# Attention and the transposes of q on quarters of the TensorE array, with a new order in the front of a fused attention, MoE and MLP kernel

## The chip, the cores and the metric

The kernel runs on one core of a Trainium2 chip. Its time is the device time of one execution in microseconds, the median of several runs. Engine names: TensorE (PE in the rows, its weight loads PEld), VectorE (DVE), ScalarE (ACT), GpSimd (POOL), SyncE (SP), which here only starts transfers.

## What is computed

Three layers in a row. A linear attention without softmax, with a norm over each head's 64 outputs; its result, 2304 rows of 512, goes into a mixture of 8 experts, two for each row, and that into an MLP with a squared ReLU.

```python
kv = einsum('bhsd,bhse->bhde', k, v)           # 4 batches, 8 heads, 576 rows, 64 columns
out = einsum('bhsd,bhde->bhse', q, kv)
x = out / sqrt(mean(out * out, -1) + 1e-6) * g_norm
logits = x @ w_gate                            # x as 2304 x 512
noisy = logits + log1p(exp(x @ w_noise)) * noise
top2 = the two largest of 8; their softmax weights
y[rows of e] += weight * (relu(x @ w1[e]) @ w2[e])
out = (s * relu(y @ w_in) ** 2 + b) @ w_out
```

## The kernel before

The order of every engine's instructions is the order of the program: nothing moves them. The front (everything up to line 747) does the attention and the gating of the first half of the rows; the main part (from line 1041) does the expert and MLP products in steps, each an `l1` (lines 789 to 791), an `l2` (813 to 815) and the side work of that step.

The 2304 rows lie in 18 tiles of 128, each made of two halves of 64 rows (`TILES`), tiles 0 to 8 from batches 0 and 1, tiles 9 to 17 from batches 2 and 3. Two tiles make a chunk, and the last of each half is alone: ten chunks, numbered 0 to 9, chunks 4 and 9 with one tile.

For a batch, `kv` multiplies k and v in pieces of 64x64, alternating over the quarters of the array, and sums over the halves in two PSUM tiles. The sums are copied to `kvc` (326, 327), and from there to the diagonal blocks of `kvbd` (`kv_diag`), which was set to zero before. `mfold_a` transposes `kvc`, and `mfold_b` multiplies the result by the gate weights, so that 16 gate columns stand behind the 64 of each head (358, 360). Thus the attention product of a tile gives 8 heads of 80 columns.

For a tile, `q_tr` brings q's columns onto the partitions by products with the identity (380) and copies the result to `qT`, even tiles on ScalarE (386), odd ones on VectorE (384). `att` multiplies it by `kvbd`, two heads at once over 128 partitions, 160 columns (397). `evict` copies the result to `x` (411). `squares` and a sum on VectorE give each head's sum of squares (418, 421). `inv_rms` takes Ln and Exp on ScalarE (429, 430). `norm` makes one Newton step on it, scales the gate columns, sums them over the heads into the logits `lg`, and scales the rest to `xn` (439 to 450). `put_rows` writes `xn` to DRAM. Chunk c's norm is issued in the round of chunk c+1.

Loads of q, k, v, the stores of `xn` and the loads of weights are all started from SP in program order. `advance(n)` loads and splits weight units up to n: `w1h` and `w2h` on ScalarE (141, 148), `w1l` on VectorE (143), `w2l` on GpSimd (149).

When the first half's logits are there, `chain` holds the generator `gating(0)`. Each `tick()` placed in the front's code runs it on to its next `yield`, a yield of n waiting n ticks: the noise (472 to 476), two choices of the best expert in three steps each, the ranks by a product, one-hots (513), the table of the first 256 rows of expert 0 (519, `idx_e` 523), two gathers of rows on GpSimd (182), and `put_x`, which transposes them (367) and splits them into `xh` on ScalarE and `xl` on VectorE (370, 371). With these, group 0's first `l1` can run. The gating of the second half lies in the first steps of the main part.

Of the kernel before, what the change touches and what calls it, by code (L numbers as in the profile page):

```python
# [21 lines left out]
def kernel(  # L22
# [188 lines left out]
    small = [(fps, "tr", 4)]  # L211
# [25 lines left out]
    def warm(n):  # L237
        ps = small_ps([P, KC, P])
        for _ in range(n):
            nc.tensor.matmul(ps, lhsT=onesb, rhs=onesb[:, None, :].to_broadcast([P, KC, P]), start=True, stop=True)  # L240
# [72 lines left out]
    def kv(b, a0=0, a1=2):  # L313
# [10 lines left out]
        if a1 == 2:  # L324
            KVP[b] = kvc = pool.tile([P, 2, 2, D], F32, name="kvc", bufs=1)
            nc.scalar.activation(kvc[:, :, 0], ps[0], AF.Copy)
            nc.vector.tensor_copy(kvc[:, :, 1], ps[1])

    def kv_diag(b):
        kvc = KVP[b]  # L330
        for m in range(2):
            r = slice(m * D, (m + 1) * D)
            dst = kvbd[b][r, :, :, m, :D]
            if m == 0:
                nc.scalar.activation(dst, kvc[r], AF.Copy)
            else:
                nc.vector.tensor_copy(dst, kvc[r])


    def mfold_a(b):  # L340
        kvc = KVP[b]
# [5 lines left out]
        kv_diag(b)  # L347
        KVP[b] = kvT

    def mfold_b(b):  # L350
# [4 lines left out]
        for m in range(2):  # L355
            r = slice(m * D, (m + 1) * D)
            if m == 0:
                nc.scalar.activation(kvbd[b][r, :, :, m, D:], pm[r, :, m], AF.Copy)
            else:
                nc.vector.tensor_copy(kvbd[b][r, :, :, m, D:], pm[r, :, m])  # L360
# [14 lines left out]
    def q_tr(t):  # L375
        pt = small_ps([P, 2, 2, P])
        for i, (b, j) in enumerate(TILES[t]):
            for a in range(2):
                for m in range(2):
                    nc.tensor.matmul(pt[m * D:(m + 1) * D, i, a, :], lhsT=KQV[b, "q"][:, 2 * a + m, j, :], rhs=ident,  # L380
                                     start=True, stop=True)
        qT = pool.tile([P, 2, 2, P], F32, name="qT", bufs=3)
        if t % 2:
            nc.vector.tensor_copy(qT, pt)
        else:
            nc.scalar.activation(qT, pt, AF.Copy)
        QT[t] = qT

    def att(t):
        qT = QT.pop(t)  # L390
        ps = fps.tile([P, 2, 512], F32, name="att", bufs=2)
        pv = ps[:, :, :H // 2 * HW_].rearrange("p a (m i c) -> p a m i c", m=2, i=2)
        for a in range(2):
            for i in range(2):
                for s_, (b, _) in enumerate(TILES[t]):
                    r = slice(s_ * HP, (s_ + 1) * HP)
                    nc.tensor.matmul(pv[r, a, :, i, :], lhsT=qT[:, s_, a, i * HP:(i + 1) * HP], rhs=kvbd[b][:, a, i],
                                     start=True, stop=True)
        AT[t] = ps[:, :, :H // 2 * HW_].rearrange("p a (h c) -> p a h c", h=H // 2)


    CHUNKS = []
    for t0 in (0, NT0):
        CHUNKS += [(t, min(2, t0 + NT0 - t)) for t in range(t0, t0 + NT0, 2)]

    def evict(c, i):
        t0, n = CHUNKS[c]
        if i == 0:
            XC[c] = (pool.tile([P, 2, H, HW_], F32, name="x", bufs=3),)
        x, = XC[c]  # L410
        nc.scalar.activation(x[:, i].rearrange("p (a h) c -> p a h c", a=2), AT.pop(t0 + i), AF.Copy)
        tick()

    def squares(c):
# [4 lines left out]
        ss = pool.tile([P, 2, H], F32, name="ss", bufs=3)  # L419
        tick()  # L420
        nc.vector.tensor_reduce(ss[:, :n], sq[:, :n], axis=AX, op=OP.add)
        tick()
        XC[c] = (x, ss)

    def inv_rms(c):
        x, ss = XC[c]
        n = CHUNKS[c][1]
        y = pool.tile([P, 2, H], F32, name="iv", bufs=3)
        nc.scalar.activation(y[:, :n], ss[:, :n], AF.Ln, scale=1.0 / D, bias=eps)
        nc.scalar.activation(y[:, :n], y[:, :n], AF.Exp, scale=-0.5)  # L430
        XC[c] = (x, ss, y)

    def norm(c):
        x, ss, y = XC.pop(c)
        t0, n = CHUNKS[c]
        x, ss, y = x[:, :n], ss[:, :n], y[:, :n]
# [31 lines left out]
    def gate_noise(g):  # L468
# [9 lines left out]
        yield 3  # L478
# [30 lines left out]
    def early_table(t0, t1, b0, b1, out, add=None):  # L509
# [5 lines left out]
        yield 6  # L515
# [11 lines left out]
    def gate_rank(g):  # L527
# [12 lines left out]
        if g == 0:  # L540
# [3 lines left out]
            yield 12  # L544
# [28 lines left out]
    def gating(g):  # L573
# [3 lines left out]
        yield 4  # L577
# [124 lines left out]
    for nm in "kv":  # L702
        load(2, nm)
    mfold_a(0)
    load(2, "q")
# [4 lines left out]
    KV_AT = {2: 1, 6: 2, 11: 3}  # L710
    LOADS = {3: (3, "kv"), 8: (3, "q")}

    for c, (t0, n) in enumerate(CHUNKS):
        for i in range(n):
            t = t0 + i
            att(t)
            if t - 1 in KV_AT:
                mfold_a(KV_AT[t - 1])
            if t + 2 < NT:
                q_tr(t + 2)  # L720
            if t - 1 in KV_AT:
# [6 lines left out]
            if t in LOADS:  # L728
                b, nms = LOADS[t]
                for nm in nms:  # L730
                    load(b, nm)
# [356 lines left out]
```

## Time and profile before

| | us |
|---|---|
| median of 3 runs | 992.24 (990.45 to 992.96) |
| the profiled execution, its own time | 993.61 |
| its span | 991.9 |
| TensorE busy | 950.9 (96%) |
| VectorE busy | 534.1 (54%) |
| ScalarE busy | 386.8 (39%) |
| GpSimd busy | 107.2 (11%) |

[...] The span is the time from the first to the last instruction; the execution's own time is 1.7 us longer.

### The profile page before, as it was taken

What the parts mean: (1) busy time and instruction counts of PE and PEld (TensorE: products, weight loads), DVE (VectorE), ACT (ScalarE), POOL (GpSimd) and SP (SyncE); (2) the same over time, 40 slices, a digit from 0 to 9 for tenths busy, and PEclk for the clock granted to TensorE, in tenths of its full rate; (3) what the DMA queues carried; (4) which work ended last, traced back from release to release, by engine and by line L of the source; (5) the groups of instructions that cost most, each with busy time, mean ns of one, the idle gap of its engine ahead of it and who ended that gap; (6) DMA issues with size and microseconds to landing.
All of it is one profiled execution on the core that took longest, in us unless ns stands there. A gap on an engine that the chain in (4) does not pass through costs nothing.

```text
span 991.9 us, 14894 instructions
## 1 busy us (share of the span) xinstructions
PE 950.9 (96%) x5874; PEld 822.8 (83%) x5875; DVE 534.1 (54%) x981; ACT 386.8 (39%) x685; POOL 107.2 (11%) x122
## 2 busy tenths in 40 slices
PE   7866999999999999999999999999999999999997
PEld 5755877989999999999999998788788878887885
DVE  2578776544676776767545455444443443444332
ACT  2554334234564555555435434222222322222221
POOL 2002325101000100100000121100110010000000
PEclk8995999999999999999999999999999999999999
DMA  9644577537476674764645541200130021001001
GB/s 333 244 164 168 175 218 239 171 107 234 138 220 215 222 272 153 228 219 155 216 142 199 170 143 50 63 1 11 32 86 1 22 74 32 1 1 43 1 1 42
DMA packets 99420, 129.14 MB, mean 130 GB/s; under 512 B 7920, under 2 KB 62192, under 8 KB 99344
## 3 DMA queue, kind: packets, MB, share of 16 engines
q1 hardware_dynamic: 91952, 108.03, 33.1%
q0 software_dynamic: 6176, 20.08, 6.9%
q8 instruction: 47, 0.77, 0.3%
q10 hardware_dynamic: 1216, 0.03, 0.1%
q14 instruction: 29, 0.24, 0.1%
HBM read 92.98 MB, written 35.13 MB: 129 GB/s over the span
## 4 chain that ended last, share of the span: by engine, by line
PE 76%; DVE 1%; ACT 1%; issue 0%; ACTq 0%
PE ph L790 13%; PE ph L791 13%; PE ph L789 12%; PE y L813 12%; PE y L814 12%; PE y L815 12%; PE sps L367 2%; DVE r L799 0%; ACT hh L801 0%; ACT r L798 0%; DVE xl L371 0%; DVE r L800 0%; DVE hl L802 0%; DVE rows L822 0%; ACT xh L370 0%
## 5 line engine op out<-in xcount | busy, mean ns | idle before, releaser
L790 PE MATMUL ph<-xl,w1h 128*128 128x320 f32 (+3 forms) x832 | 278.1, 334 | 2.9 <-DVE xl L371 2.7
L789 PE MATMUL ph<-xh,w1h 128*128 128x320 f32 (+3 forms) x832 | 277.7, 334 | 2.0 <-ACT xh L370 1.2
L791 PE MATMUL ph<-xh,w1l 128*128 128x320 f32 (+3 forms) x832 | 277.5, 334 | 0.0
L813 PE MATMUL y<-w2h,hh 128*128 128x512 f32 x608 | 242.4, 399 | 2.6 <-ACT hh L801 1.7
L815 PE MATMUL y<-w2h,hl 128*128 128x512 f32 x608 | 237.9, 391 | 0.0
L814 PE MATMUL y<-w2l,hh 128*128 128x512 f32 x608 | 237.7, 391 | 0.0
L790 PEld LDWEIGHTS ph<-xl,w1h 128*128 128x128 f32 x832 | 157.9, 190 | 18.6 <-DVE xl L371 5.1
L789 PEld LDWEIGHTS ph<-xh,w1h 128*128 128x128 f32 x832 | 158.0, 190 | 18.1 <-ACT xh L370 3.4
L791 PEld LDWEIGHTS ph<-xh,w1l 128*128 128x128 f32 x832 | 157.9, 190 | 9.9
L799 DVE SCALAR_TENSOR_TENSOR r<-ph,r 128x512 f32<-128x512 f32 (+1 forms) x80 | 51.0, 638 | 177.6 <-ACT r L798 176.1
L793 ACT ACTIVATE hh<-ph 128x320 fp32r<-128x320 f32 (+2 forms) x128 | 55.9, 437 | 230.6 <-PE ph L791 220.0
L794 DVE SCALAR_TENSOR_TENSOR hl<-ph,hh 128x320 fp32r<-128x320 f32 (+2 forms) x128 | 62.5, 490 | 142.3 <-ACT hh L793 136.2
L815 PEld LDWEIGHTS y<-w2h,hl 128*128 128x128 f32 x608 | 114.1, 188 | 25.7 <-DVE hl L802 0.6
L813 PEld LDWEIGHTS y<-w2h,hh 128*128 128x128 f32 x608 | 114.4, 188 | 23.8 <-ACT hh L801 2.4
L814 PEld LDWEIGHTS y<-w2l,hh 128*128 128x128 f32 x608 | 114.4, 188 | 20.3
L798 ACT ACTIVATE r<-ph 128x512 f32<-128x512 f32 (+1 forms) x80 | 44.3, 554 | 189.6 <-PE ph L791 183.9
L801 ACT ACTIVATE hh<-r 128x512 fp32r<-128x512 f32 (+1 forms) x80 | 47.1, 589 | 101.8 <-DVE r L800 97.9
L802 DVE TENSOR_TENSOR hl<-r,hh 128x512 fp32r<-128x512 f32 (+1 forms) x80 | 51.2, 639 | 52.5 <-ACT hh L801 50.3
L182 POOL DMA_INDIRECT rows<-xs,idx x35 | 34.9, 998 | 314.0 <-PE sps L367 176.5
L182 POOL DMA_INDIRECT rows<-ys,slot_i x36 | 34.8, 968 | 272.0 <-DVE rows L771 133.1
L143 DVE SCALAR_TENSOR_TENSOR w1l<-raw,gcol,w1h 128x512 fp32r<-128x512 f32 x64 | 47.8, 748 | 24.5 <-ACT w1h L141 19.9
L148 ACT ACTIVATE w2h<-raw 128x512 fp32r<-128x512 f32 x80 | 49.7, 621 | 2.3 <-DMA raw<-in_moe_w_dram 2.3
(166 smaller groups left out, 809.2 us busy)
## 6 DMA issues: line engine op xcount, KB each, us to landing
raw<-in_moe_w_dram SPq DMA_DIRECT2D x128, 256.0 KB
ys<-rows SPq DMA_DIRECT2D x40, 256.0 KB
c_raw<-in_moe_w_in_dram SPq DMA_DIRECT2D x16, 512.0 KB
c_raw<-in_moe_w_out_dram SPq DMA_DIRECT2D x16, 512.0 KB
wd<-c_fl SPq DMA_DIRECT2D x16, 512.0 KB
raw<-wd SPq DMA_DIRECT2D x32, 256.0 KB
ys<-zero SPq DMA_DIRECT2D x13, 512.0 KB
q<-in_q_dram SPq DMA_DIRECT2D x4, 1152.0 KB
```

Source lines behind the costliest of these rows:

```text
L148: nc.scalar.activation(h2, r2, AF.Copy)
L182: nc.gpsimd.indirect_dma_start(out=dst, out_offset=None, in_=src, in_offset=bass.IndirectOffsetOnAxis(ap=icol, axis=0))
L789: nc.tensor.matmul(ps[:, :wd], lhsT=w1h[:, c, :], rhs=xh[:, c, cs], start=c == 0, stop=False)
L790: nc.tensor.matmul(ps[:, :wd], lhsT=w1h[:, c, :], rhs=xl[:, c, cs], start=False, stop=False)
L791: nc.tensor.matmul(ps[:, :wd], lhsT=w1l[:, c, :], rhs=xh[:, c, cs], start=False, stop=c == KC - 1)
L793: nc.scalar.activation(hh[:, cs], ps[:, :wd], AF.Relu)
L794: nc.vector.scalar_tensor_tensor(hl[:, cs], ps[:, :wd], 0.0, hh[:, cs].bitcast(F32), op0=OP.max, op1=OP.subtract)
L799: nc.vector.scalar_tensor_tensor(r[:, :wd], ps[:, :wd], 0.0, r[:, :wd], op0=OP.max, op1=OP.mult)
L802: nc.vector.tensor_sub(hl[:, cs], r[:, :wd], hh[:, cs].bitcast(F32))
L813: nc.tensor.matmul(y, lhsT=hh[:, cs], rhs=w2h, start=f == 0, stop=False)
L814: nc.tensor.matmul(y, lhsT=hh[:, cs], rhs=w2l, start=False, stop=False)
L815: nc.tensor.matmul(y, lhsT=hl[:, cs], rhs=w2h, start=False, stop=f == nf - 1)
```

## The change

Four things. First, `att` and `q_tr` also work on 64x64 pieces: the state is kept as `kvg` without zero blocks, a product takes one head's 64 partitions and 80 columns, and the transposes take 64 rows of q each, so that each product of before becomes two. Second, `q_tr` does both tiles of a chunk, two chunks ahead, with one copy on ScalarE. Third, the copies of the key-value state move between the engines: both `kvc` copies and both fold copies are ScalarE's, and VectorE copies the sums straight from PSUM in `kv_put`. A part of the Newton step goes to GpSimd. Fourth, the round of a chunk has a new order, ticks and yields differ, and three weight units are split in the front instead of four. PSUM is shared out anew: two small tiles instead of four, and two banks for the transposes.

```diff
-    small = [(fps, "tr", 4)]
+    small = [(fps, "tr", 2)]
...
-    kvbd = []
-    for b in range(B):
-        t = pool.tile([P, 2, 2, 2, HW_], F32, name=f"kvbd{b}")
-        nc.gpsimd.memset(t, 0.0)
-        kvbd.append(t)
+    kvg = [pool.tile([P, 2, 2, HW_], F32, name=f"kvg{b}") for b in range(B)]
...
+            for i in range(2):
+                nc.scalar.activation(kvc[:, :, i], ps[i], AF.Copy)
+            KVP[b] = ps, kvc
+
+    def kv_put(b):
+        for i in range(2):
+            nc.vector.tensor_copy(kvg[b][:, :, i, :D], KVP[b][0][i])
...
-            if m == 0:
-                nc.scalar.activation(kvbd[b][r, :, :, m, D:], pm[r, :, m], AF.Copy)
-            else:
-                nc.vector.tensor_copy(kvbd[b][r, :, :, m, D:], pm[r, :, m])
+            nc.scalar.activation(kvg[b][r, :, :, D:], pm[r, :, m], AF.Copy)
...
+    def q_tr(c):
+        if c >= NCH:
+            return
+        t0, n = CHUNKS[c]
+        pt = fps.tile([P, 2, 2, 2, 2, HP], F32, name="qtp", bufs=1)
+        for u in range(n):
+            for s_, (b, j) in enumerate(TILES[t0 + u]):
+                for a in range(2):
+                    for m in range(2):
+                        for i in range(2):
+                            r = slice(i * HP, (i + 1) * HP)
+                            nc.tensor.matmul(pt[m * D:(m + 1) * D, i, u, s_, a, :], lhsT=KQV[b, "q"][r, 2 * a + m, j, :],
+                                             rhs=ident[r, r], start=True, stop=True)
+        qT = pool.tile([P, 2, 2, 2, 2, HP], F32, name="qT", bufs=3)
+        fl = "p i u s a t -> p i u (s a t)"
+        nc.scalar.activation(qT.rearrange(fl)[:, :, :n], pt.rearrange(fl)[:, :, :n], AF.Copy)
+        QT[c] = qT
...
+                    for m in range(2):
+                        r = slice(m * D, (m + 1) * D)
+                        nc.tensor.matmul(pv[s_ * HP:(s_ + 1) * HP, m, a, i, :], lhsT=QT[c][r, i, u, s_, a, :],
+                                         rhs=kvg[b][r, a, i, :], start=True, stop=True)
...
+    def sums(c):
+        x, sq = XC[c]
+        n = CHUNKS[c][1]
+        ss = pool.tile([P, 2, H], F32, name="ss", bufs=2)
+        nc.vector.tensor_reduce(ss[:, :n], sq[:, :n], axis=AX, op=OP.add)
+        w = pool.tile([P, 2, H], F32, name="iw", bufs=2)
+        nc.gpsimd.tensor_scalar(w[:, :n], ss[:, :n], -0.5 / D, -0.5e-6, op0=OP.mult, op1=OP.add)
         tick()
...
-        nc.vector.tensor_scalar(ss, ss, -0.5 / D, -0.5e-6, op0=OP.mult, op1=OP.add)
         nc.vector.tensor_mul(u, y, y)
+        nc.vector.tensor_mul(u, u, w)
         tick()
-        nc.vector.tensor_mul(u, u, ss)
...
-        yield 3
+        yield 2
...
-        yield 6
+        yield 3
...
-            yield 12
+            yield 11
...
-        yield 4
+        yield 2
...
-    KV_AT = {2: 1, 6: 2, 11: 3}
-    LOADS = {3: (3, "kv"), 8: (3, "q")}
+    KV_AT = {3: 1, 7: 2, 11: 3}
...
-        for i in range(n):
-            t = t0 + i
-            att(t)
-            if t - 1 in KV_AT:
-                mfold_a(KV_AT[t - 1])
-            if t + 2 < NT:
-                q_tr(t + 2)
-            if t - 1 in KV_AT:
-                mfold_b(KV_AT[t - 1])
-            if c and i == 0:
-                inv_rms(c - 1)
-            evict(c, i)
-            if t in KV_AT:
-                kv(KV_AT[t])
...
-            if c and i == n - 1:
-                norm(c - 1)
-            if 12 <= t < 16:
-                advance(t - 11)
-            elif t == 11:
-                advance(0)
...
-        squares(c)
-        put_rows()
+        new = None
+        for u in range(n):
+            att(c, u)
+            evict(c, u)
+            if u == 0:
+                inv_rms(c - 1)
+            if t0 + u in KV_AT:
+                new = KV_AT[t0 + u]
+                kv(new)
+        squares(c)
+        q_tr(c + 2)
+        if new:
+            kv_put(new)
+            mfold_a(new)
+        norm(c - 1)
+        put_rows()
+        sums(c)
+        if new:
+            mfold_b(new)
+        if c == 1:
+            for nm in "kv":
+                load(3, nm)
+        if c == 2:
+            load(3, "q")
+        if c and sum(CHUNKS[c - 1]) == NT0:
+            chain[:] = [gating(0), 0]
+        if c >= 6:
+            advance(c - 6)
```

## Rows read from the trace of the kernel before

**Rows 1.** Busy time by stretch: PE, PEld, DVE, ACT, POOL, granted clock, DMA share, GB/s.
```profile
14.00:61.00 47.00, 39.14 (x866) 35.23 (x864) 25.78 (x55) 23.55 (x50) 0.68 (x2) 0.96 0.77 279
61.00:96.00 35.00, 21.54 (x214) 16.67 (x206) 27.81 (x67) 16.74 (x33) 7.25 (x6) 0.67 0.43 142
96.00:991.90 895.90, 880.85 (x4643) 765.56 (x4643) 477.83 (x844) 344.96 (x600) 92.02 (x89) 0.99 0.38 119
```

**Rows 2.** Waits from 14 to 96 us: total us, times, longest.
```profile
ACT iv L429 <- DVE ss L421: 22.0, 8, 6.0
...
PE att L397 <- ACT x L411: 9.4, 5, 2.5
```

**Rows 3.** Timeline, an undisturbed round: start, us, engine, instruction, [idle before].
```profile
37.11 0.31 ACT L429 ACTIVATE iv<-ss,eps 128x16 f32<-128x16 f32 x1 [1.13 <-DVE ss L421]
...
38.03 0.17 DVE L440 TENSOR_TENSOR iu<-iv 128x16 f32<-128x16 f32 x1
...
40.75 1.22 DVE L421 TENSOR_REDUCE ss<-sq 128x16 f32<-128x1024 f32 x1
42.00 0.31 ACT L429 ACTIVATE iv<-ss,eps 128x16 f32<-128x16 f32 x1 [0.87 <-DVE ss L421]
```

**Rows 4.** Groups by line, 14 to 96 us: count, busy us, mean ns, idle before.
```profile
L411 ACT ACTIVATE x<-att 128x640 f32<-128x640 f32 x18 | 12.2, 690 | 0.0
...
L384 DVE COPY qT<-sps 128x512 f32<-128x512 f32 x9 | 6.2, 689 | 9.0 <-PE sps L380 9.0
L386 ACT ACTIVATE qT<-sps 128x512 f32<-128x512 f32 x9 | 5.4, 595 | 8.2 <-PE sps L380 8.2
```

**Rows 5.** Timeline of ScalarE, a square and two copies of a kv.
```profile
38.88 1.06 ACT L418 ACTIVATE sq<-x 128x1024 f32<-128x1024 f32 x1
...
43.05 0.27 ACT L326 ACTIVATE kvc<-sps 128x128 f32<-128x128 f32 x1
45.28 0.38 ACT L346 ACTIVATE kvT<-sps 128x256 f32<-128x256 f32 x1 [1.96 <-PE sps L344]
```

**Rows 6.** Timeline of TensorE: q_tr, att, kv.
```profile
24.19 1.09 PE L380 MATMUL sps<-ident,q 128*64 128x128 f32 x16 [0.46 <-DMA q<-in_q_dram]
...
35.15 1.28 PE L397 MATMUL att<-kvbd,qT 128*64 128x160 f32 x16
36.24 1.07 PE L380 MATMUL sps<-ident,q 128*64 128x128 f32 x16
...
40.42 2.33 PE L322 MATMUL sps<-v,k 64*64 64x64 f32 x144
...
74.02 2.40 PE L397 MATMUL att<-kvbd,qT 128*64 128x160 f32 x16 [2.52 <-ACT x L411]
```

**Rows 7.** Timeline, the noise of gating: its first and last operation.
```profile
58.68 0.25 ACT L472 ACTIVATE g<-lg 128x72 f32<-128x72 f32 x1
...
59.81 0.34 POOL L476 TENSOR_TENSOR g<-g,lg 128x72 f32<-128x72 f32 x1
```

**Rows 8.** Timeline of VectorE, gating and weights, and one GpSimd operation.
```profile
65.20 0.23 DVE L490 TENSOR_TENSOR g<-g,m_all 128x72 f32<-128x72 f32 x1
...
74.61 0.75 DVE L143 SCALAR_TENSOR_TENSOR w1l<-raw,gcol,w1h 128x512 fp32r<-128x512 f32 x1 [1.10 <-ACT w1h L141]
75.28 1.25 DVE L439 TENSOR_SCALAR ss<-ss 128x16 f32<-128x16 f32 x1
...
77.42 2.88 DVE L513 TENSOR_SCALAR ohe<-io,early 128x256 f16<-128x256 f16 x9
...
75.17 1.32 POOL L149 TENSOR_TENSOR w2l<-raw,w2h 128x512 fp32r<-128x512 f32 x1 [7.46 <-ACT w2h L148]
```

**Rows 9.** Timeline, the end of the front: gather, transposes, first product on xl.
```profile
88.05 1.08 POOL L182 DMA_INDIRECT rows<-xs,idx_e  x1 [0.17 <-DVE iu L440]
...
93.52 1.11 PE L367 MATMUL sps<-ident,rows 128*128 128x128 f32 x4 [0.52 <-DMA rows<-xs,idx_e]
...
96.04 0.58 PE L790 MATMUL ph<-xl,w1h 128*128 128x256 f32 x1
```

More of the change, by code (lines that the diff above doesn't have):

```diff
@@ L237, in warm @@
     def warm(n):
-        ps = small_ps([P, KC, P])
+        ps = fps.tile([P, KC, P], F32, name="warm", tag="att", bufs=2)
         for _ in range(n):
@@ L324, in kv @@
         if a1 == 2:
[L325 to L333, printed above, removed]
-            if m == 0:
-                nc.scalar.activation(dst, kvc[r], AF.Copy)
-            else:
-                nc.vector.tensor_copy(dst, kvc[r])
+            kvc = pool.tile([P, 2, 2, D], F32, name="kvc", bufs=1)
+            for i in range(2):
[4 more added lines that the diff above has]
+            nc.vector.tensor_copy(kvg[b][:, :, i, :D], KVP[b][0][i])
     def mfold_a(b):
-        kvc = KVP[b]
+        kvc = KVP[b][1]
         pt = small_ps([P, 2, P])
@@ L346, in mfold_a @@
         nc.scalar.activation(kvT, pt, AF.Copy)
-        kv_diag(b)
         KVP[b] = kvT
@@ L356, in mfold_b @@
             r = slice(m * D, (m + 1) * D)
-            if m == 0:
-                nc.scalar.activation(kvbd[b][r, :, :, m, D:], pm[r, :, m], AF.Copy)
-            else:
-                nc.vector.tensor_copy(kvbd[b][r, :, :, m, D:], pm[r, :, m])
+            nc.scalar.activation(kvg[b][r, :, :, D:], pm[r, :, m], AF.Copy)
     X = {0: tuple(gp.tile([P, KC, EB * P], F32R, name=n) for n in ("xh0", "xl0"))}
@@ L373, with att @@
     QT, AT, XC, XO = {}, {}, {}, []
[L375 to L392, printed above, removed]
+    CHUNKS = []
+    for t0 in (0, NT0):
+        CHUNKS += [(t, min(2, t0 + NT0 - t)) for t in range(t0, t0 + NT0, 2)]
+    NCH = len(CHUNKS)
+    def q_tr(c):
[15 more added lines that the diff above has]
+        QT[c] = qT
+    def att(c, u):
+        t = CHUNKS[c][0] + u
+        ps = fps.tile([P, 2, 512], F32, name="att", tag="att", bufs=2)
+        pv = ps[:, :, :H // 2 * HW_].rearrange("p m (a i c) -> p m a i c", a=2, i=2)
         for a in range(2):
@@ L395, in att, with evict @@
                 for s_, (b, _) in enumerate(TILES[t]):
[L396 to L406, printed above, removed]
+                    for m in range(2):
+                        r = slice(m * D, (m + 1) * D)
+                        nc.tensor.matmul(pv[s_ * HP:(s_ + 1) * HP, m, a, i, :], lhsT=QT[c][r, i, u, s_, a, :],
+                                         rhs=kvg[b][r, a, i, :], start=True, stop=True)
+        AT[t] = pv.rearrange("p m a i c -> p m a (i c)")
+    def evict(c, u):
         t0, n = CHUNKS[c]
-        if i == 0:
+        if u == 0:
             XC[c] = (pool.tile([P, 2, H, HW_], F32, name="x", bufs=3),)
-        x, = XC[c]
-        nc.scalar.activation(x[:, i].rearrange("p (a h) c -> p a h c", a=2), AT.pop(t0 + i), AF.Copy)
-        tick()
+        x = XC[c][0][:, u].rearrange("p (a m i) c -> p m a (i c)", a=2, m=2)
+        nc.scalar.activation(x, AT.pop(t0 + u), AF.Copy)
     def squares(c):
@@ L701 @@
     kv(0, 1, 2)
-    for nm in "kv":
+    kv_put(0)
+    for nm in "kvq":
         load(2, nm)
     mfold_a(0)
-    load(2, "q")
     q_tr(0)
```

30 lines of the change are left out of this document (14 added, 16 removed).

## The prediction

> **What bounds the kernel now.** I read the granted clock and span first, then busy time by stretch, then the waits, and last the engines' timelines of the front. Two stages with different limits stand out [rows 1]. From 96 us on TensorE is busy 880.85 of 895.9 us: the expert and MLP products run back to back, the change touches none of them, and so nothing is to be won there. Before 96 us it is busy 39.14 of 47.0 and then 21.54 of 35.0 us, at a mean granted clock of 0.67 in the second stretch. The front ends when the rows of group 0 are split into xh and xl and the first l1 product that reads xl starts, at 96.04 [rows 9]. What the change is worth is how far this moment moves; it then carries over one to one, as long as nothing behind it waits for something that didn't move too.
>
> In the front TensorE isn't the engine that ends last. ScalarE waits 22.0 us in all in front of inv_rms for VectorE's sums, and TensorE's att waits 9.4 us for the eviction that is queued behind that inv_rms [rows 2]. The undisturbed round of a chunk is a circle over two engines [rows 3]: sums end, Ln and Exp on ScalarE, norm on VectorE, the next sums, the next Ln. From Ln at 37.11 to Ln at 42.00 it takes 4.89 us: 0.92 to the first multiply of norm (38.03), 3.94 from there to the end of the sums (41.97). The qT copy, the kv copies, gating and the weight splits are queued in between and lengthen it.
>
> **The change part by part.**
> *Quarters.* Per tile, att was 16 instructions in 1.28 us and the transposes 16 in 1.07 us [rows 6], 2.35 together. Now each is 32 instructions on 64x64 pieces, of 80 and 64 columns. The nearest row is kv, which already runs in the same alternation of quarters: 144 instructions with 64 columns in 2.33 us, 16.2 ns each. That gives 32 x 16.2 = 0.52 us for the transposes and, scaled by the columns that are loaded and streamed (144/128), 0.58 us for att: 1.1 us for a tile, 2.2 for a chunk. Bounds: 2.2 at full clock, 4.4 at half (att took 2.40 us at 74.02, after 2.52 us of idling, against 1.28). The saving of some 1.25 us a tile, 22 us in all, is almost all off the path: in a round of 4.8 us TensorE was no bound, and it gets more idle time.
>
> [...]
>
> *Copies of q.* One ScalarE copy of 1024 columns for two tiles takes the place of alternating copies of 512, 0.689 us on VectorE and 0.595 on ScalarE [rows 4]. Its cost lies between 1.06 (the square of 1024 columns, [rows 5]) and 2 x 0.595 = 1.19; I take 1.06. VectorE loses 9 x 0.69 = 6.2 us, of which 5 x 0.69 = 3.5 lie after 61 us, where VectorE is the busiest engine (27.81 of 35 us, [rows 1]). ScalarE then has per chunk two evictions at 0.69, Ln (0.31, [rows 3]) and Exp (taken as 0.22), square and copy at 1.06: 4.0 us, inside the round, so its copies cost nothing while the round is VectorE's. The cover is thin (0.8 us), and gone in the three chunks with a kv.
>
> [...]
>
> *Key-value state.* The zeroed kvbd, its diagonal copies and one fold copy on VectorE go; ScalarE does both kvc copies (0.27 each, [rows 5]) and both fold copies; VectorE does the two kv_put copies of the same size, ahead of norm, while it waits for Ln and Exp. The long stop, VectorE standing in front of norm until the fold was copied, goes. In its place kv_put waits for kv alone, and norm is queued behind it.
>
> *Orders.* evict(c,0) now goes ahead of inv_rms(c-1), so att's first buffer comes free early. q_tr(2) comes into chunk 0 and waits for the second batch's q, whose transfer TensorE waited for until 24.19 [rows 6]; the issue order on SP up to it is unchanged, so that time stays, and att of chunk 1 is now queued behind it. Later loads move on SP: the k and v of batch 3 go behind the store of chunk 0, its q to chunk 2; both stand free of their use by over 5 us by the sum below. On GpSimd the new weight operation sits ahead of Exp's end and hides. Gating's ticks now stand in norm and sums alone, and its yields are shorter: counted through, the noise and the first choice both fall into the norm that runs in chunk 6, the index into that of chunk 8, put_x into the last norm. One weight unit less is split in the front.
>
> *The sum, from 24.19.* TensorE has by then idled some 4 us, so I take q_tr(2) and att of chunk 1 at half clock (2.1 + 2.3) and kv(1) at full, 2.33: 31.0. Two kv_put 0.55, norm and sums 3.94: chunk 1 done at 35.5. ScalarE meanwhile: kvc 0.55, square 1.06, q copy 1.06, kvT 0.38 [rows 5], fold 0.6 and its copies 0.45 (estimates: short products, two copies under 0.27), att 0.6, eviction 0.69: Ln at 36.35, 0.85 late. Then 0.9 and 3.94: chunk 2 at 41.15, and an undisturbed round: chunk 3 at 46.0. There kv(2) pushes ScalarE to 47.2; chunks 4 and 5 have one half-size step each (I take six tenths of 3.94 for one with everything half): 51.5 and 55.3.
> Chunk 6: from Ln, ScalarE has Ln, Exp, two kvc, eviction, square, q copy and kvT, 4.2 us, and only then the noise, 1.47 us from its first operation to the end of GpSimd's add [rows 7]. VectorE stands in the middle of norm until 61.0; this is the new wait. Three choice steps of two operations at about 0.27 (0.23 and the gap, [rows 8]) and the rest of norm and sums, 2.86: 65.4. Chunk 7: 0.9 + 3.94 + two choice steps: 71.3. Then one-hots 2.88, the two operations before them 0.45, one w1l 0.75 [rows 8]: 75.35. Chunk 8: 3.94, the index 0.15, and 0.6 for VectorE being held while GpSimd does a w2l (the 0.16 us scaling took 1.25 at 75.28, beside the w2l of 75.17): 80.0. Chunk 9, half a sum: 0.9 + 3.4: 84.3. Last norm up to the tick 0.9 + 0.9, and two xl of 0.69: 87.5. The w1l in chunks 8 and 9 lie in the 0.9 us of waiting for Ln and Exp.
> The gather is not last: index at 77, and from the first gather's start to the second block's transposes it was 88.05 to 93.52, 5.5 us [rows 9]: 82.6, before 86.
> So the start moves from 96.04 to 87.5, 8.5 us. Back goes 0.7 for the unit that is now split in step 0, whose w1l (0.75) lies ahead of a VectorE that gating keeps busy there. **7.8 us** remain. The profiled run took 993.61 us with a span of 991.9; on it that is 985.8, and on the median, 992.24, it is **984.4**.
>
> The ends: nothing at half clock (2.2 less), no holding (0.6), unit hidden (0.7) gives a gain of 11.3. kv(1) and part of kv(2) at half clock too (2.35 + 1.5), each of three w2l costing a full 1.1 (2.7 more), 0.3 more in step 0 gives about 1. Hence 980.9 to 991.
>
> **Rivals.**
> 1. *The gain is taken back at once.* If TensorE meets a wait behind group 0 that didn't move, the time stays at 990 to 992. For it: gating of the second half and the gather of group 1 lie in the first eight steps, and VectorE is near full there. Against it: all of that starts from the logits of the last chunks, which come earlier too, and DMA is only 0.43 busy before 96 us [rows 1]. It would equally come to this if the handoffs I count as hidden add up to 0.5 us in each of ten chunks.
> 2. *The quarters don't overlap* (slower; also the case in which the change doesn't do what it says). If each of the 64 instructions of a tile costs what one of the sixteen costs now, 1.07/16 = 67 ns, a tile takes 4.3 us. From 24.19 sixteen tiles 69, three kv with their folds 10, gating's products 2, the end 3: 108, 12 us later than 96.04, so 1004. It decides from about 54 ns an instruction. Against it stand the 16.2 ns of kv.
> 3. *TensorE at half clock throughout.* A chunk is then 4.4 us, just under the round; with kv at 4.7 more, chunks 1, 3 and 6 lengthen. 24.19 on, that adds 4 to 5 us to the sum: 988 to 989.
>
> **How the numbers follow.** Forecast with its own range, 980 to 987.5: 0.68; rival 3: 0.14; rival 1: 0.12; rival 2: 0.04; other losses 0.02. A measurement of this kernel tells about 0.3% (3 us) from no change. Faster by that holds the forecast and rival 3, 0.82; the same 0.12; slower 0.06. The range 979.5 to 991 takes in rivals 1 (its better half) and 3 and the bounds above.
>
> **What would show it.** Right: att and transposes at 16 to 20 ns an instruction; sums following each other in 4.8 us in chunks 2 and 3; VectorE waiting for GpSimd's add in chunk 6 for some 4 us; the first l1 product on xl near 87.5, and the stretch behind it as long as before. Wrong: instructions at 50 ns and more; ScalarE without a gap and VectorE waiting for Exp in every chunk; xh waiting for gathered rows; or TensorE idling in the steps of groups 0 and 1.

## The result, and the profile after

| | before | after |
|---|---|---|
| median, us | 992.6 (990.45 to 993.43) | 1002.23 (999.0 to 1003.38) |
| profiled execution, its span | 993.61, 991.9 | 999.0, 997.3 |
| first l1 product on xl, in the profile ([rows 9] for before) | 96.04 | 99.94 |
| from there to the end | 895.86 | 897.36 |

The ratio is 1.0095 [1.0066, 1.0125]: slower by 0.95%, where 0.8% faster was forecast and the range ended at 991.0. The profiled execution is the shortest of the four of after, so its rows show 5.4 us of the loss: 3.9 in the front, 1.5 behind it. The other 4.2 us between the medians stand in no trace.

The busy time by stretch of after, cut at other moments than [rows 1] because the front ends later; columns as there (the granted clock is a share of the full one):

```profile
14.00:66.00 52.00, 34.97 (x1322) 31.51 (x1325) 19.46 (x40) 25.91 (x49) 1.01 (x5) 0.80 0.68 245
66.00:100.00 34.00, 15.12 (x338) 12.10 (x328) 26.38 (x66) 17.89 (x38) 9.02 (x12) 0.69 0.50 160
100.00:997.30 897.30, 878.76 (x4643) 764.76 (x4643) 476.91 (x837) 346.05 (x600) 92.15 (x90) 0.99 0.38 119
```

TensorE is busy 35 of the first 52 us, VectorE 19.5, ScalarE 26: no engine is full, and yet the stretch is longer. The waits of after from 14 to 98 us say what stands between them (they answer [rows 2]; columns as there):

```profile
DVE kvg L328 <- ACT kvc L323: 15.9, 3, 8.3
...
ACT iv L431 <- DVE ss L419: 11.4, 6, 3.8
ACT x L406 <- PE att L396: 10.5, 7, 2.4
...
PE sps L318 <- issue: 6.7, 3, 4.9
PE att L396 <- issue: 6.4, 4, 2.6
...
PE qtp L380 <- issue: 2.4, 2, 2.2
```

The two waits of [rows 2] have changed as the forecast had it: inv_rms waits 11.4 us for VectorE's sums instead of 22.0, and att waits only 0.4 us for evictions. The reverse has come instead, evictions that wait 10.5 us for att, and VectorE stands 15.9 us in `kv_put` (its first operation is kvg). Behind these are three rows that end in "issue", 15.5 us together: there TensorE stood still in front of kv, att and the transposes and waited for nothing that the profile shows. In before the same view has only these two (L354 is mfold_a, L397 is att):

```profile
PE sps L354 <- issue: 1.8, 1, 1.8
...
PE att L397 <- issue: 0.4, 1, 0.4
```

TensorE's timeline of after shows where it stops. Here "64*64" is the piece of the array, "x10" the number of products, and the last column the idle time before them:

```profile
24.80 1.99 PE L380 MATMUL qtp<-ident,q 64*64 64x64 f32 x64
26.53 1.80 PE L396 MATMUL att<-kvg,qT 64*64 64x80 f32 x52
30.94 0.42 PE L396 MATMUL att<-kvg,qT 64*64 64x80 f32 x10 [2.61 <-issue]
31.14 0.21 PE L318 MATMUL sps<-v,k 64*64 64x64 f32 x1
31.15 0.23 PE L396 MATMUL att<-kvg,qT 64*64 64x80 f32 x1
31.15 0.27 PE L318 MATMUL sps<-v,k 64*64 64x64 f32 x2
31.21 0.25 PE L396 MATMUL att<-kvg,qT 64*64 64x80 f32 x1
31.22 3.24 PE L318 MATMUL sps<-v,k 64*64 64x64 f32 x113
35.04 0.62 PE L318 MATMUL sps<-v,k 64*64 64x64 f32 x26 [0.59 <-issue]
...
41.18 0.79 PE L396 MATMUL att<-kvg,qT 64*64 64x80 f32 x32
...
44.37 0.35 PE L396 MATMUL att<-kvg,qT 64*64 64x80 f32 x3 [1.38 <-issue]
44.49 2.08 PE L318 MATMUL sps<-v,k 64*64 64x64 f32 x124
51.48 0.59 PE L318 MATMUL sps<-v,k 64*64 64x64 f32 x19 [4.91 <-issue]
```

The stops fall in the middle of att and of kv, where no product needs anything new. Count the products from one stop to the next: from 30.94 to 35.04 it is 10+1+1+2+1+113 = 128; from 44.37 to 51.48 it is 3+124 = 127. Between 35.04 and 44.37 there are 255 (not all of them shown), two such portions, and no stop at the seam. A product is two instructions here, a weight load and a matmul (the page of after counts 6451 and 6450), so a portion is 256 instructions.

The page of each profile says the same from the other side. Its head counts the instructions, and its list of DMA queues has two of the kind "instruction" (packets, MB, share of 16 engines): q14 with 29 packets in both profiles, and q8. Before:

```profile
span 991.9 us, 14894 instructions
...
q8 instruction: 47, 0.77, 0.3%
```

After:

```profile
span 997.3 us, 16031 instructions
...
q8 instruction: 51, 0.84, 0.3%
```

The 576 products more of the change are 1152 instructions, 4.5 portions of 256, and q8 has four packets more, of some 16 KB each (0.84 MB in 51). In windows of 0.2 us the trace also tells when each packet was moved. In after, the one for the longest stop has this row in the window from 49.0 to 49.2:

```profile
q8 instruction: 1, 0.02, 30.2%
```

The packets stand in a fixed relation to the ends of the stops (in after; the last row of the table is before; the DMA share is that of the stretch from the begin to the packet or, in the first three rows, to the end of the stop, in rounded windows):

| portion before begins | packet moved | stop ends | begin to packet | packet to end | DMA share |
|---|---|---|---|---|---|
| 23.89 | 28.5 | 30.94 | 4.6 | 2.4 | 1.05 |
| 30.94 | 32.7 | 35.04 | 1.8 | 2.3 | 0.21 |
| 44.37 | 49.1 | 51.48 | 4.7 | 2.4 | 1.01 |
| 17.60 | 21.4 | 23.89 | 3.8 | 2.5 | 1.06 |
| 51.48 | 53.4 | no stop | 1.9 | | 0.98 |
| | 29.5 | 31.96 (mfold_a) | | 2.5 | |

So a stop ends 2.3 to 2.5 us after the next packet has been moved. The packet is moved 1.8 us after the portion before it began to run where the queues carry little (0.21 up to the end of the stop, though 0.50 up to the packet), and 3.8 to 4.7 us after where the share is 1.01 to 1.06; but once, at 0.98, only 1.9 us after, so that the share alone doesn't set it. The portions of 128 quarter products run for 2.1 us each at full clock (128 x 16.2 ns; 127 took 2.18 from 44.4 to 46.6, at a granted clock of 1.00), but in the first and third rows they come 7 us apart, and in the second 4. That is 30 to 55 ns a product. A product of 128x64 took 67 to 80 ns [rows 6] (at a granted clock of 1.00 from 35.15 to 37.30 in before), and so stayed behind its supply. In after the supply stopped TensorE for 15.5 us.

### The profile page after: what moved, and what is told of

The parts are those of the page before. It is cut to its first block, busy times and chain, and to the rows that moved or that the text cites. A ratio compares the mean times of both kernels' runs of the same rounds, so it can differ in the third digit from the quotient of the medians.

```text
span 997.3 us, 16031 instructions
## 1 busy us (share of the span) xinstructions
PE 937.1 (94%) x6450; PEld 812.8 (82%) x6451; DVE 525.3 (53%) x958; ACT 391.6 (39%) x690; POOL 107.1 (11%) x128
## 4 chain that ended last, share of the span: by engine, by line
PE 76%; DVE 1%; ACT 1%; issue 0%; ACTq 0%
PE ph L792 13%; PE ph L793 12%; PE ph L791 12%; PE y L815 12%; PE y L816 12%; PE y L817 12%; PE sps L354 2%; DVE r L801 0%; DVE xl L358 0%; ACT hh L803 0%; ACT r L800 0%; DVE r L802 0%; DVE hl L804 0%; DVE rows L824 0%; ACT xh L357 0%
## 5 line engine op out<-in xcount | busy, mean ns | idle before, releaser
L793 PEld LDWEIGHTS ph<-xh,w1l 128*128 128x128 f32 x832 | 157.3, 189 | 13.2 <-DVE w1l L143 3.3
L800 ACT ACTIVATE r<-ph 128x512 f32<-128x512 f32 (+1 forms) x80 | 44.4, 555 | 187.7 <-PE ph L793 187.7
```

The costliest lines, as they stand in the source:

```text
L793: nc.tensor.matmul(ps[:, :wd], lhsT=w1l[:, c, :], rhs=xh[:, c, cs], start=False, stop=c == KC - 1)
```

## The experiments

The theory is now that the supply of instructions stops TensorE; its rival is that the new orders lose the time by waits of their own. Each kernel's ratio is to the kernel before on the same chip; "front" is the moment of the first l1 product that reads xl, 96.04 before and 99.94 after.

**One part alone.** e1_orders keeps the orders of after and puts att and the transposes back on 128x64 pieces, with the zeroed state (and two buffers for xn):

```diff
-            nc.vector.tensor_copy(kvg[b][:, :, i, :D], KVP[b][0][i])
+            for m in range(2):
+                r = slice(m * D, (m + 1) * D)
+                nc.vector.tensor_copy(kvbd[b][r, :, i, m, :D], KVP[b][0][i][r])
...
-        pt = fps.tile([P, 2, 2, 2, 2, HP], F32, name="qtp", bufs=1)
+        pt = fps.tile([P, 2, 2, 2, P], F32, name="qtp", bufs=1)
...
+                        nc.tensor.matmul(pt[m * D:(m + 1) * D, u, s_, a, :], lhsT=KQV[b, "q"][:, 2 * a + m, j, :],
+                                         rhs=ident, start=True, stop=True)
...
+                    nc.tensor.matmul(pv[s_ * HP:(s_ + 1) * HP, a, :, i, :], lhsT=QT[c][:, u, s_, a, i * HP:(i + 1) * HP],
+                                     rhs=kvbd[b][:, a, i], start=True, stop=True)
```

> The changed kernel's orders, copies and ticks, but att and q_tr in the form of before (half as many products, on 128x64 pieces, with the zeroed kvbd; xn has two buffers instead of three, and the state takes four VectorE copies instead of two). Theory of the instruction pages (TensorE stands still at every 128th product because its next 256 instructions aren't there yet): its idle time that is put down to issue before 98 us falls from 15.5 us to under 5, the first l1 product on xl comes at 88 to 92 us instead of 99.9, the time is 988 to 992. Rival, the new orders and ScalarE's copies lose the time: the first l1 product on xl stays at 98 us or later, and the time at 1000 or more.

Measured: 1.0054 [1.0031, 1.0077], front 97.40. The stops are nearly gone, 3.5 us in all, but the front comes only 2.5 us earlier. Its waits from 14 to 98 us and one row of TensorE's timeline say what took their place:

```profile
ACT qT L387 <- PE qtp L384: 10.3, 4, 4.8
...
DVE iu L444 <- ACT iv L433: 8.2, 4, 6.5
```

```profile
33.79 3.29 PE L384 MATMUL qtp<-ident,q 128*64 128x128 f32 x29 [2.56 <-issue]
```

29 of the transposes of two tiles took 3.29 us, at a mean granted clock of 0.53 (33.79 to 37.1), ScalarE's copy of them waited for it with everything queued behind the copy, inv_rms too, and VectorE waited for inv_rms. So half a per cent is lost with half as many of these products, and the stops of after aren't the whole loss. But a stop of 2.56 us heads this chain too, so that what the orders lose by themselves isn't separated here. Of the expectation only the stops came true; the front was to come by 92, or in the rival not before 98 with a time of 1000 or more.

e4_before_quarters is the converse, the kernel before with att and the transposes in quarters:

```diff
+        pf = fps.tile([P, 2, 512], F32, name="qtp", bufs=1)
...
+                        nc.tensor.matmul(pt[m * D:(m + 1) * D, i, s_, a, :], lhsT=KQV[b, "q"][r, 2 * a + m, j, :],
+                                         rhs=ident[r, r], start=True, stop=True)
...
+                        nc.tensor.matmul(pv[s_ * HP:(s_ + 1) * HP, m, a, i, :], lhsT=qT[r, i, s_, a, :],
+                                         rhs=kvbd[b][r, a, i, m, :], start=True, stop=True)
```

> The kernel before with its order and copies, only att and q_tr on quarters (twice as many products; PSUM shared out as two small tiles and two banks for the transposes). Pages: idle time put down to issue before 96 us rises from about 2 us to over 8, and the time is 996 to 1003. Rival, the quarters are free and the orders lose the time: issue stays under 4 us, and the time is 988 to 993.

Measured: 1.0044 [1.0025, 1.0063], front 102.71. Its stops are 9.3 us between 14 and 88 us, in five places. But the largest wait of TensorE there belongs to the experiment and not to the change: with `bufs=1` there is a single buffer for one tile's transposes, which waits for VectorE's copy.

```profile
PE qtp L383 <- DVE qT L387: 9.2, 3, 6.8
```

So it shows that the stops come with the quarters, in the order of before too (9.3 us instead of 2.2); how much of its 0.44% is theirs, it doesn't tell.

**Are the stops tied to the count?** e8_shift issues eight warm-up products more ahead of everything:

```diff
-    warm(14)
+    warm(22)
```

> The changed kernel with eight more warm-up products ahead of everything (22 instead of 14), nothing else. Theory of the instruction pages: TensorE's stops lie at fixed places of its instruction stream, every 256 instructions from its start, so each moves 8 products forward: the first transposes stop after 49 instead of 57 products, the first att after 45 instead of 53, kv of batch 2 earlier by 8 too. Rival, the stops belong to places of the program (the first use of a PSUM bank, of a quarter, an operand that comes late): they stay after 57, 53, 52 and 124 products.

Measured in a single execution: 999.42, front 100.52. TensorE's timeline, to be laid beside that of after:

```profile
25.67 1.86 PE L396 MATMUL att<-kvg,qT 64*64 64x80 f32 x44
30.67 0.93 PE L396 MATMUL att<-kvg,qT 64*64 64x80 f32 x18 [3.13 <-issue]
...
44.84 0.42 PE L396 MATMUL att<-kvg,qT 64*64 64x80 f32 x10 [1.94 <-issue]
45.04 0.28 PE L318 MATMUL sps<-v,k 64*64 64x64 f32 x4
45.10 0.23 PE L396 MATMUL att<-kvg,qT 64*64 64x80 f32 x1
45.11 2.70 PE L318 MATMUL sps<-v,k 64*64 64x64 f32 x112
51.68 1.01 PE L318 MATMUL sps<-v,k 64*64 64x64 f32 x27 [3.88 <-issue]
```

Att stops behind its 44th product instead of its 52nd, kv(2) with 27 products left instead of 19: each of these two stops has moved eight products forward in the program, and 10+4+1+112 is again 127. The other two that were expected, in the first transposes after 49 products and in the first att after 45, didn't occur. A wait for data, for a buffer or for another engine would have stayed at its product. That the portions set the places of the stops is shown.

**Does the length come from the transfers?** e6_noload leaves out the loads of batches 2 and 3 and works on the data of batches 0 and 1 in their place:

```diff
-    for nm in "kvq":
-        load(2, nm)
+        KQV[2, nm], KQV[3, nm] = KQV[0, nm], KQV[1, nm]
...
-        if c == 1:
-            for nm in "kv":
-                load(3, nm)
-        if c == 2:
-            load(3, "q")
```

> The changed kernel without the loads of q, k and v for batches 2 and 3; their work is done on the data of batches 0 and 1 (so that part of the result is left out). TensorE has the same instructions. Pages that come slowly because the same DMA engines are full: idle time put down to issue falls from 15.5 us to under 8, none is over 3 us, the first l1 product on xl comes by 93 us. Rival, a page takes its time whatever else moves, or the stops come from the array itself: issue stays at 12 us or more.

Measured in a single execution: 992.92, front 90.30. Two of its stops, and the busy times of the stretch between them (the share before the last number is that of DMA):

```profile
27.97 0.42 PE L396 MATMUL att<-kvg,qT 64*64 64x80 f32 x10 [1.28 <-issue]
31.79 0.62 PE L318 MATMUL sps<-v,k 64*64 64x64 f32 x26 [1.69 <-issue]
```

```profile
28.00:31.80 3.80, 2.11 (x129) 1.97 (x129) 0.00 (x0) 0.70 (x1) 0.00 (x0) 1.00 0.02 4
```

With DMA at 0.02 a portion comes every 3.8 us and no stop is over 2.2, where after had 4.9; the stops are still 10.2 us together. The sum lies between what was expected (under 8) and the rival (12 or more); the longest stop and the front came as expected. So by these rows there are two parts, as an estimate: some 2 us for each portion that runs at 16 ns a product with the queues empty (stops of 1.28 and 1.69 in the rows above, at a share of 0.02 in between), and up to some 3 us more where they are full (4.91 in after, at a share of 1.01). The front, 9.6 us earlier, is an upper bound for the second part, since waits for the loaded data go too. Behind it 3.5 us are given back: the rest of the span is 900.9 us, in after 897.4.

e13_loads keeps the loads and issues k and v of batch 3 ahead of the first store, which was to get them through before kv(2):

```diff
+        if c == 1:
+            for nm in "kv":
+                load(3, nm)
         norm(c - 1)
         put_rows()
         sums(c)
         if new:
             mfold_b(new)
-        if c == 1:
-            for nm in "kv":
-                load(3, nm)
```

> The changed kernel with one thing moved: k and v of batch 3 are ordered ahead of chunk 0's store instead of behind it, so that they go through while the queues stood empty (31 to 39 us) and not from 40 us on, beside the next store and q. If a page of instructions comes late because these transfers fill the DMA engines, the stop in kv of batch 2 (4.9 us) falls under 2.5 and chunk 3 is done 2 to 4 us earlier than 56.8; the ratio to before is 1.004 to 1.008 instead of 1.0095. Rival, pages take their time whatever else moves: the stop stays over 4 us and the ratio at 1.009.

Measured: 1.0088 [1.0071, 1.0104], front 102.58 (its profiled execution, 1009.25 us, is the longest of its five). The stops did not become shorter as a whole: 15.2 us, in after 15.5. TensorE's rows and most of the stretch between them in three windows:

```profile
46.57 0.39 PE L396 MATMUL att<-kvg,qT 64*64 64x80 f32 x2 [2.56 <-issue]
...
53.95 0.80 PE L318 MATMUL sps<-v,k 64*64 64x64 f32 x19 [3.80 <-issue]
```

```profile
46.60:48.00 1.40, 1.40 (x51) 1.40 (x54) 0.00 (x0) 0.78 (x2) 0.00 (x0) 0.50 1.02 253
48.00:50.00 2.00, 2.00 (x88) 2.00 (x82) 0.00 (x0) 0.00 (x0) 0.00 (x0) 0.56 0.97 325
50.00:52.00 2.00, 0.15 (x9) 0.01 (x1) 0.00 (x0) 0.00 (x0) 0.00 (x0) 1.00 0.65 249
```

The edit failed to do what it was made for: q of batch 3 (issued at 45.45) and two stores kept the DMA share at 0.97 and more until 50, and at 0.65 until 52. The packet was moved at 51.5, as the queues ran empty (0.01 from 52 to 54), 4.9 us after the portion before it had begun, and the stop ended 2.45 later. It is 3.80 us long instead of 4.91 because that portion ran at a granted clock of 0.50 to 0.56. The expectation was missed, and the reading of e6 is neither confirmed nor contradicted: the transfers would have to be gone when a portion is due, and nothing in the program tells SP when that is. The opposite case, transfers moved onto a portion, came with e14_weights below.

**Single mends of the orders.** e15_ahead takes the transposes one chunk ahead instead of two, with kv a tile earlier:

```diff
-    q_tr(1)
...
-    KV_AT = {3: 1, 7: 2, 11: 3}
+    KV_AT = {2: 1, 6: 2, 11: 3}
...
-        q_tr(c + 2)
+        q_tr(c + 1)
...
-        if c == 2:
+        if c == 3:
             load(3, "q")
```

> The changed kernel with q_tr one chunk ahead instead of two and kv behind the first att of its chunk; q of batch 3 one chunk later. Chunk 1's att and kv stand no longer behind the second batch's q. Expected: chunk 1 done at 36 to 38 us instead of 40.5, first l1 on xl 2 to 4 us earlier, ratio 1.004 to 1.008. Rival, the pages alone set the front, and the stops only move: ratio 1.009 or more.

Measured: 1.0073 [1.0055, 1.0090], front 98.25, stops 9.0 us. Chunk 1's sums end at 36.36 instead of 40.47, since att and kv of that chunk no longer stand behind transposes of a q that is still on its way; of these 4.1 us only 1.7 are left at the end of the front. The ratio's interval overlaps that of after.

e7_u4 and e14_weights split four weight units in the front again, because the first step behind it stood 3.1 us for the fourth one:

```diff
-        if c >= 6:
-            advance(c - 6)
+        if c == 6:
+            advance(1)
+        if c > 6:
+            advance(c - 5)
```

That is e7_u4; e14_weights also orders the loads of the first two units in chunk 4 already (`advance(0)` splits none):

```diff
-        if c >= 6:
-            advance(c - 6)
+        if c == 4:
+            advance(0)
+        if c >= 6:
+            advance(c - 5)
```

> The changed kernel with four weight units split in the front, as before, instead of three. If w1l of unit 3 costs what the profile shows in step 0 (3.1 us in front of the first l1 of that unit), the time falls by 2 to 3 us, to 999 to 1000, and that wait is gone; if something else is late there anyway, it stays at 1001 to 1003.

> The changed kernel with the first two weight units ordered in chunk 4 and four units split in the front. The wait of 3.1 us for w1l in step 1 goes; ScalarE, which waited 6.7 us for the weights where only the split was moved forward, doesn't wait. Expected 2 to 4 us: ratio 1.005 to 1.008. Rival, the split in the front costs there what it saves behind: ratio 1.008 to 1.011, first l1 on xl at 101 or later.

Measured: 1.0089 [1.0061, 1.0117] with the front at 104.25, and 1.0083 [1.0065, 1.0101] with 103.96. The wait of 3.1 us is gone in both, and the front pays for it. In e7_u4 ScalarE, with Ln and Exp of chunk 6 and the evictions of chunk 7 queued behind it, waits for the raw weights:

```profile
ACT w1h L141 <- DMA raw<-in_moe_w_dram: 6.7, 1, 6.7
```

In e14_weights ScalarE no longer waits for them, but VectorE stands 6.9 us for the noise instead of 4.5. The cause is a stop again. At the same place of att, in chunk 6, after has the first of these rows and e14_weights the second; the last one is VectorE's wait in e14_weights:

```profile
67.99 0.42 PE L396 MATMUL att<-kvg,qT 64*64 64x80 f32 x10 [1.57 <-issue]
```

```profile
70.50 0.42 PE L396 MATMUL att<-kvg,qT 64*64 64x80 f32 x10 [3.48 <-issue]
...
DVE m_all L492 <- POOL g L479: 6.9, 1, 6.9
```

ScalarE's eviction waits for this att (3.9 us) with the noise queued behind it. The portion before began at 64.27 and 64.86, at a granted clock of 1.00 in both. In after the DMA share was 0.10 then, and the packet came 1.1 us later; in e14_weights the four loads of the weights, started from 62.34 to 64.83, had the share at 0.99, and it came 2.8 us later. e7_u4, which orders them later, has 1.29 us there. So in these executions, at one place of the program, transfers that no product needed yet made the stop 1.9 us longer. This is the test that e13 was meant to be, in the other direction.

**All mends together.** e11_tuned_quarters is after with the three single mends (the transposes one chunk ahead, k and v of batch 3 early, four units as in e14_weights), and with the noise started half a round sooner and the new weight operation back on VectorE for the last chunks, where GpSimd is busy with the gathers:

```diff
+        if c and sum(CHUNKS[c - 1]) == NT0:
+            chain[:] = [gating(0), 0]
         sums(c)
...
-        yield 2
+        yield 3
...
-        nc.gpsimd.tensor_scalar(w[:, :n], ss[:, :n], -0.5 / D, -0.5e-6, op0=OP.mult, op1=OP.add)
+        (nc.vector if c >= 8 else nc.gpsimd).tensor_scalar(w[:, :n], ss[:, :n], -0.5 / D, -0.5e-6, op0=OP.mult, op1=OP.add)
```

e10_tuned_full has the same edits with att and the transposes on 128x64 pieces (with the zeroed state, as in e1_orders), e12_tuned_attq with att on quarters and the transposes on 128x64.

> The same mended order with att and q_tr on quarters, as in the change. Pages: twice the products in the same front, issue idle over 9 us, first l1 on xl 3 to 7 us later than in the kernel with 128x64 pieces, ratio to before 0.995 to 1.003. Rival, quarters are free once nothing is queued behind the late q: as early as or earlier than the other, ratio under 0.99.

> The form of before for att and q_tr (128x64 pieces) in the changed kernel's order, with the places mended where the profile shows waits: q_tr one chunk ahead instead of two (so chunk 1's att and kv stand no longer behind the second batch's q), kv behind the first att of its chunk, k and v of batch 3 ordered ahead of the first store, weights 0 and 1 ordered in chunk 4 and four units split in the front, the noise issued in the sums of chunk 5 instead of in the next norm, the last two small weight operations on VectorE. Expected: chunk 1 done by 33 us, issue idle under 5 us, first l1 product on xl at 86 to 91 us, no wait for w1l in step 1, ratio to before 0.990 to 0.997. Rival, the order itself (copies on ScalarE) costs the time: ratio 1.003 or more.

> The same mended order with att on quarters and q_tr on 128x64 pieces: half of the added products. Pages: between the two, issue idle 5 to 9 us, first l1 on xl 1 to 4 us later than with both on 128x64 pieces. Rival: it lies outside, earlier than both.

| | ratio to before | front | stops, us |
|---|---|---|---|
| e11, both on quarters | 0.9990 [0.9973, 1.0006] | 95.42 | 8.5 |
| e10, none | 0.9976 [0.9957, 0.9996] | 94.28 | none listed |
| e12, att alone | 0.9960 [0.9942, 0.9979] | 92.12 | 5.6 |

The orders, mended, give back about one per cent (1.0095 to 0.9990 with both on quarters), though none of e7, e13, e14 and e15 gave more than some 0.2, and the interval of each overlaps that of after. With the order mended, quarters and 128x64 pieces can't be told apart, since their intervals overlap. Nor do the 8.5 us of stops in e11 bring its front more than 1.1 us behind that of e10, which has none: a stop costs time only where the path waits for it. Att alone in quarters has the best middle value, but its interval overlaps the others too. Much of what was expected of these three was missed: e11's front was to be 3 to 7 us behind e10's, e10's was to come by 91, and e12's front came ahead of e10's, as its rival had it.

**A version that beats both.** In e12 the gathered rows are transposed by 88.28, but ScalarE's xh is queued behind Ln and Exp of chunk 9, which wait 4.48 us for VectorE's sums until 89.23:

```profile
89.67 1.06 ACT L357 ACTIVATE xh<-sps 128x512 fp32r<-128x512 f32 x2
```

e16_putx takes three ticks away, so that `put_x` stands ahead of them:

```diff
-            yield 11
+            yield 8
```

> The mended order with att on quarters and q_tr on 128x64 pieces, and put_x issued in the sums of chunk 9 instead of in the norm behind it: xh no longer stands behind Ln and Exp of chunk 9, which wait for those sums. First l1 on xl 1 to 2.5 us earlier than 92.1, if the gathered rows are there at 88; ratio to before 0.993 to 0.996. Rival, the rows are late and VectorE's last norm waits behind xl: no earlier, ratio 0.996 or more.

Measured: 0.9955 [0.994, 0.997], 990.57 against 995.5 on the same chip; its profiled execution, 986.19 us, is the shortest of its six. Its busy times by stretch:

```profile
14.00:66.00 52.00, 35.81 (x1110) 31.57 (x1110) 24.96 (x57) 29.98 (x58) 1.89 (x8) 0.97 0.76 271
66.00:88.55 22.55, 13.44 (x247) 10.68 (x247) 20.03 (x47) 14.84 (x29) 7.05 (x7) 0.68 0.54 176
88.55:984.50 895.95, 880.26 (x4643) 765.86 (x4643) 476.85 (x842) 345.40 (x601) 92.99 (x90) 0.99 0.38 120
```

TensorE is at a clock of 0.97 in the first stretch, and its front, which ends at 88.55, is 7.5 us shorter than before's, close to the 8.5 that the prediction gave to after, and the rest of the span is as long as before's, 895.95 and 895.86. The median gains 4.9 us, less than this shortest execution. Of the 3.6 us by which its front is shorter than e12's, 1.1 were there already when the index of the gather was computed (79.00 instead of 80.09), and so don't come from the ticks. It still has 7.2 us of stops. Against e12 the intervals overlap, so what the three ticks bring isn't settled; that e16 is faster than before and after is.

## Why the prediction was wrong, step by step

**The bound, and what the change is worth: right in the main.** The main stage is untouched, and what the first l1 on xl gained carried over, in e16 to 0.1 us. It isn't sure to: behind the front after lost 1.5 us more, and e12, whose front was 3.9 us shorter than before's, gave back 2.5 there (the rest of its span is 898.4). That is the first rival, in part.

**The quarters: the step that failed.** On the profiled executions the forecast missed by 13.2 us (985.8 and 999.0), 12.4 of them in the front. The price of an instruction was right where the instructions were there: att of a tile, 32 products, in 0.79 us at 41.18, hence by estimate some 0.6 without the 0.21 that a single product takes (31.14), for 0.58 forecast. Wrong was to take a rate from 144 products, hardly more than one portion, for a stream of 1728, and to call TensorE's part "almost all off the path". The reader of the profile could have seen it: [rows 2] leaves out the two "issue" rows of before, 2.2 us, and the instruction queue stands on the page.

The sum can now nearly be closed. Forecast and measured ends of the sums (the end of each chunk's reduce on VectorE):

| | forecast | measured | round longer by |
|---|---|---|---|
| chunk 1 | 35.5 | 40.47 | 5.0 |
| chunk 2 | 41.15 | 45.61 | -0.5 |
| chunk 3 | 46.0 | 56.81 | 6.35 |
| chunk 5 | 55.3 | 66.09 | 0 |
| first l1 on xl | 87.5 | 99.94 | 1.65 |

Chunk 3's 6.35 us are the two stops in front of its kvc, 1.38 and 4.91 = 6.29. Of chunk 1's 5.0, 3.2 are stops (2.61 and 0.59); kv(1) ran at a lower clock, 3.9 us from 31.14 without its stop instead of 2.33 (the mean granted clock from 31 to 35 us is 0.57), 1.6 more; and q came 0.6 later, while the transposes and att took 0.6 less than the 4.4 at half clock. That makes 4.8 of 5.0. So by this account 9.5 of the 12.4 us by which the front missed its forecast are stops. That they weren't made up later is the other half of the mistake: VectorE stands in front of `kv_put`, with norm queued behind it, so that each stop in kv lies on the path. The forecast had named this wait, and priced it as if kv never stopped. Where no stop falls, the round came out near its forecast: 5.14 us to the end of chunk 2's sums, against 4.89 in [rows 3].

**From chunk 5 on: nearly right, in part by luck.** 32.2 us were forecast, 33.85 measured, 36.0 in before. The new wait for the noise was 4.5 us where some 4 were forecast, but a stop of 1.57 us, which the forecast didn't have, lies ahead of it. The last rows of VectorE below show 1.0 for the weight operation on GpSimd that is queued behind the gathers (forecast as hidden) and operations that take 1.13 instead of 0.17 (for which 0.6 was forecast, once). ScalarE's copies of q took 1.00 to 1.06, as forecast.

```profile
72.91 0.23 DVE L492 TENSOR_REDUCE m_all<-g 128x9 f32<-128x72 f32 x1 [4.52 <-POOL g L479]
...
91.93 0.18 DVE L444 TENSOR_TENSOR iu<-iu,iw 128x16 f32<-128x16 f32 x1 [1.02 <-POOL iw L421]
92.14 1.13 DVE L446 SCALAR_TENSOR_TENSOR iv<-iu,iv 128x16 f32<-128x16 f32 x1
```

**The unit split in step 0: mis-sized.** 0.7 us were taken off; TensorE stood 3.1 (the span behind the front grew by 1.5).

```profile
111.84 0.39 PE L793 MATMUL ph<-xh,w1l 128*128 128x256 f32 x1 [3.13 <-DVE w1l L143]
```

Splitting it in the front didn't help as it was done here: in e7_u4 and e14_weights the front came 4 us later.

**The rivals.** The second had the sign and, by chance, nearly the time: 1004 and 54 ns an instruction, for 1002.23 and a supply of 30 to 55. Its mechanism didn't happen: 32 quarter products of att took 0.79 us (41.18), where a single one takes 0.23 (31.15), so they overlapped. Its chance of 0.04 rested on the kv row alone, and the range of the *Quarters* term reached only from full to half clock: a supply of instructions was no bound of it. The third, TensorE at half clock (a granted clock of 0.50 in before from 74.02 to 76.40, where att took 2.40 us), is a part of the loss (mean granted clock of after 0.69 from 66 to 100 us, but 0.80 from 14 to 66), and its share isn't separated. Behind the stop of 4.91 us the granted clock was 0.57 (51.48 to 53.5) and 0.50 (to 57.0), where it had been 1.00 from 44.4 to 46.6; but it was 0.56 from 24.8 to 28.3 too, ahead of the stop of 2.61 us, and in e6_noload it stayed at 1.00 from 24 to 32, with stops of 1.28 and 1.69 us.

**What stays open.** How the mends share the one per cent that they give together, and how the loss of 0.95% divides between the stops and the orders: e1 and e4 each lose about half, but e4 brought a wait of its own, e1 kept a stop of 2.56 us, and the two aren't independent. A run with after's orders and transfers held back whenever a portion is due wasn't made. Why the packet of 53.4 came early beside a DMA share of 0.98 isn't known.

## What to carry to other kernels

Before cutting products into smaller ones, compare the time of 128 of them with the time between two portions of instructions: where the engine ran through a portion faster than the next one came (here in 2.1 us, with the portions 3.8 to 7 us apart), the supply set the pace, and only the part of the work that was off the path for other reasons hid it (8.5 us of stops in e11, a front 1.1 us behind that of e10). Price an instruction from a run of products that is several portions long, and read rows that end in "issue" as a resource with a rate, beside the engines and the queues. When a new order loses time, mend it as a whole: no single edit here was clear of after's interval, and all of them together gave back one per cent.

## What the runs showed of the hardware

TensorE's instructions came in portions of 256 (127 to 128 products with their weight loads, from stop to stop in after and e8_shift). A portion for which TensorE stood began 2.2 to 2.7 us after its packet was moved, in after, before, e6_noload, e8_shift, e13_loads and e16_putx alike. The packet was moved 1.1 to 1.8 us after the portion before it had begun with DMA at 0.02 to 0.21 (1.1 in e6_noload, from 27.97 to 29.1; 1.8 in after, from 30.94 to 32.7, where the share up to the packet was 0.50), and mostly 2.8 to 4.9 us with DMA at 0.93 to 1.06 (2.8 in e14_weights, 3.8 to 4.7 in after, 4.9 in e13_loads), though 1.9 once in after at 0.98. Thus transfers of data that the products at hand didn't need stopped TensorE for 1.9 us more at the one place where the same products ran with and without them (3.48 in e14_weights, 1.57 in after), and, as an estimate, for up to some 3 us more by the rows of after and e6_noload (4.91 and 1.69).
